# Attention and mixer on one core: channel weights with group scales, signs by GpSimd, norms by TensorE, and products of no use in the first batch

## The chip, the cores and the metric

The kernel runs on one core of a Trainium2 chip. The metric is device time in microseconds; each figure is a median of several runs. The core's engines are TensorE (PE in the views; PEld is its weight load), VectorE (DVE), ScalarE (ACT) and GpSimd (POOL); SyncE (SP) issues DMAs.

## What is computed

```python
def sm_attn(qq, kk, vv):                       # softmax attention, scale 1/8
    ...
q_d = q.reshape(B, H, S // 4, 4, D).mean(axis=3)      # the same for k, v
out_up = np.repeat(sm_attn(q_d, k_d, v_d), 4, axis=2)
scores = np.where(np.abs(pos[:, None] - pos[None, :]) < 4, q @ k.T / 8, -1e9)
out_local = softmax(scores) @ v
x = (out_up + out_local) as [B, S, H * D]
h = np.maximum(x^T @ w_tok1, 0) @ w_tok2
u = x + h^T
out = u + np.maximum(u @ w_ch1, 0) @ w_ch2
```

B, H, S, D are 8, 8, 576, 64, so x has 512 channels. `w_tok1` is 576x256, `w_tok2` 256x576, `w_ch1` 512x1536, `w_ch2` 1536x512. The weights are float64, all else is float32.

## The kernel before, in words

**Batches.** The eight batches run one after another. For each: queries and keys are pooled, four pairs of heads go through the pooled attention (`sd` scores, `pd`, `td` transposed, `ad` products, `od` output), five tiles of rows through the local one (`sc` scores, `P` exponentials, `mx` maxima, `r` sums, `pT` transposed, `av` products). `od` of all four pairs is written into the tile `vw` by DMAs on ACT's queue (L421), beside the windows of v, so that one `av` product adds both attentions; its result is `x`. The token mixer splits `x` into two parts (`xh`), forms `t` with W1 (five groups of six products, L105), `hid`, `t` again with W2 (L105, L545), `u`, and the maximum of `u` over all partitions (`um`: a reduction, a transpose on TensorE, a reduction, a product with ones). `u` is scaled by a power of two and split into two fp16 parts, `uh` (L567, L569). The channel mixer forms `c` from `uh` and C1, three products for the two parts each (`mm3`, L105), takes them up as `h` (relu, two fp16 parts, L644 and L646), and forms `c` from `h` and C2, which goes out as `u` (L672).

**Channel weights.** C1 and C2 have twelve tiles of 128x512 each. The chip reads float64 as pairs of 32-bit words. ACT scales the high word (L175), GpSimd rounds the low one (L178), DVE shifts the high word into it (L180) and, in `signed` (L184), ORs the sign bit in, into a tile of CW. TensorE multiplies the upper halves of the words by a matrix of ones, so that DVE (L283) finds the largest sum over a column. When all twelve tiles are there, one power of two for the whole matrix follows (`pow2`, L109 to L111), and each tile is split into a first part on ACT (L268) and a second on DVE (L270). W1 (five pieces) and W2 (four) go the same way but for the scale, and are split by L213 and L215.

**Buffers.** Raw pieces of W1, W2 and C1 share the five buffers `h`, with two loads in flight in each of the three streams; C2's raw tiles come in pairs in the two buffers `vw`, after batch 0's last `av`.

**Order.** Instructions run on each engine in the order in which the program issues them. For batch 0 and the start of batch 1, `drive` sets it: a list of streams (generators), whose steps name an engine, an estimated time and what they need. It keeps a clock for each engine and takes the earliest step that is ready, or one earlier in the list if it starts within PATIENCE of that one. From batch 1 on, the channel products are issued in fixed order, and attention and mixer of the next batch (`side`) are dealt out beside them (`tick`).

Of the kernel before, what the change touches and what calls it, by code (L numbers as in the profile page):

```python
# [10 lines left out]
U32 = mybir.dt.uint32  # L11
U8 = mybir.dt.uint8
# [4 lines left out]
NEG = -1.0e30  # L17
# [15 lines left out]
def tile_ups_attention_mixer(ctx, tc, qk, vw, vr, w1, w2, c1, c2, out):  # L33
# [14 lines left out]
    BUFS = dict(h=5, w=4, xh=3, x=5, u0=4, u1=8, uh0=4, uh1=4, qk=4, qd=1, vw=2, vd=1, pt=2, od=1, sm=10, sc=24)  # L48
# [19 lines left out]
    onesb = sb.tile([128, 128], BF16, name="onesb")  # L68
    nc.vector.memset(onesb, 1.0)
# [6 lines left out]
    masks = []  # L76
    for kind in range(3):
        m = sb.tile([128, WB], F32, name=f"mask{kind}")
        nc.gpsimd.memset(m, 0.0)
        for j in range(4):  # L80
            a = m[QB * j:QB * j + QB]
            select(a, 0, -1, 1, WB, NEG)
            select(a, 6, 1, -1, WB, NEG)
            if kind == 0 and j == 0:
                select(a, -3, 0, 1, WB, NEG)
            if kind == 2 and j == 1:
                select(a, QB + 2, 0, -1, WB, NEG)
        masks.append(m)
# [3 lines left out]
    nc.gpsimd.memset(rep, 1.0)  # L92
    for j in range(4):
        a = rep[QB * j:QB * j + QB]
        select(a, 0, 1, -4, QB // 4, 0.0)
        select(a, 3, -1, 4, QB // 4, 0.0)
# [21 lines left out]
    clock = dict.fromkeys("AGVPSD", 0.0)  # L118
# [13 lines left out]
    def fetched(nbytes):  # L132
        clock["D"] = max(clock["D"], now[0]) + nbytes / 230e3
        return clock["D"] + 2.0

    def drive(streams, until):

        items = [[g, next(g, None), 0.0] for g in streams]
        while until not in made:
# [14 lines left out]
            if e == "P" and ("uh", 0, 0) not in made:  # L154
                us *= 1.8
# [13 lines left out]
    def to_f32(raw, at):  # L169
# [6 lines left out]
        yield step("G", 0.1 + n * 0.0016)  # L176

        nc.gpsimd.tensor_scalar(lo, lo, 2.0 ** -29, -0.501, ALU.mult, ALU.add)  # L178
        yield step("V", 0.08 + n * 0.0012)
        nc.vector.scalar_tensor_tensor(lo, hi, 3, lo, ALU.logical_shift_left, ALU.bitwise_or)  # L180

    def signed(y, raw):
        words = raw.rearrange("p (n two) -> p n two", two=2)
        nc.vector.scalar_tensor_tensor(y, words[:, :, 1], 0x80000000, words[:, :, 0],  # L184
                                       ALU.bitwise_and, ALU.bitwise_or)

    def load_raw(src, n, name):
        raw = T([src.shape[0], 2 * n], U32, "h", f"{name}_raw")
        nc.sync.dma_start(raw, src)
        return raw, fetched(src.shape[0] * n * 8)  # L190

    def load_raws(srcs, name):

        t = T([128, len(srcs), 1024], U32, "vw", f"{name}_raws")
        for i, s in enumerate(srcs):
            nc.sync.dma_start(t[:, i], s)
        return [(t[:, i], fetched(2 ** 19)) for i in range(len(srcs))]

    def token_weight(pieces, fin, name):
        raws = {}  # L200
        yield step("S", 0.1)
        for i in range(min(2, len(pieces))):
            raws[i] = load_raw(*pieces[i], f"{name}{i}")
        for i, (src, n) in enumerate(pieces):
            raw, at = raws.pop(i)
            yield from to_f32(raw, at)
            yield step("V", 0.08 + n * 0.0012)
            m = raw.rearrange("p (n two) -> p n two", two=2)[:, :, 0]
            signed(m, raw)
# [6 lines left out]
            make((name, i), e)
            if i + 2 < len(pieces):
                raws[i + 2] = load_raw(*pieces[i + 2], f"{name}{i + 2}")
# [4 lines left out]
    CW = [sb.tile([128, 512], F32, name=f"CW{i}") for i in range(2 * NF + 1)]  # L223

    class Channel:


        def __init__(self, name, src, at, k, sums, pairs):
            self.name, self.src, self.at, self.k, self.sums, self.pairs = name, src, at, k, sums, pairs
            self.fin = []  # L230

        def bank_of(self, i):
            return "m" if i % (NF if self.pairs else 4) == 0 else ""

        def stage(self, *start):
            name = self.name
            yield step("S", 0.1, *start)
            if self.pairs:
                raws = load_raws(self.src[0:2], f"{name}0") + load_raws(self.src[2:4], f"{name}2")
            else:  # L240
                raws = [load_raw(self.src[i], 512, f"{name}{i}") for i in range(2)]
            self.mx = sb.tile([128, 4], F32, name=f"{name}_mx")
            for i in range(NF):
                raw, at = raws[i]
                yield from to_f32(raw, at)
                yield step("V", 0.68)
# [12 lines left out]
            self.inv = sb.tile([128, 1], F32, name=f"{name}_inv")
            self.s = sb.tile([128, 1], F32, name=f"{name}_s")  # L260
            yield step("V", 0.6, *([("C1", NF - 1)] if self.at else []))
            nc.vector.tensor_reduce(big, self.mx[:, :self.n], axis=AX.X, op=ALU.max)
            pow2(big, 2.0 ** -self.k, self.inv, self.s)
            for i in range(NF):
                y = CW[self.at + i + 1]
                f = CW[self.at + i].bitcast(F16).rearrange("p (a n) -> p a n", a=2)
                yield step("A", 0.72)
                nc.scalar.activation(f[:, 0], y, AF.Copy, scale=self.s)  # L268
                t = yield step("V", 0.75)
                nc.vector.scalar_tensor_tensor(f[:, 1], y, self.s, f[:, 0], ALU.mult, ALU.subtract)  # L270
                self.fin.append(f)
                make((name, i), t)

    def sums_c1(w, i, ab):

        if i % 4 == 0:
            w.bank = PM(f"C1_sum{i}")
        for d in range(4):
            nc.tensor.matmul(w.bank[:, 128 * (i % 4):128 * (i % 4) + 128], onesb, ab[:, 128 * d:128 * d + 128],
                             start=d == 0, stop=d == 3)  # L280
        if i % 4 == 3:
            w.n = i // 4 + 1
            return lambda: nc.vector.tensor_reduce(w.mx[:, w.n - 1:w.n], w.bank, axis=AX.X, op=ALU.max)  # L283
# [16 lines left out]
    ic = sb.tile([128, 1], F32, name="ic")  # L300
# [199 lines left out]
    def mix(st):  # L500

        b = st.b
        NT = len(TILES)

        def xf(t):
            return st.x[t].rearrange("p hp two d -> p (hp two d)")

        def split(t):
            n = TILES[t][1]
            xh = st.xh[t] = T([n, 2, 512], F32R, "xh", f"xh{b}_{t}")  # L510
            yield step("A", 0.62, ("x", b, t), *([("over", 0, 0)] if b == 1 else []))
            nc.scalar.copy(xh[:, 0], xf(t))  # L512
            yield step("V", 0.69)
# [5 lines left out]
        for t in range(NT):  # L519
# [3 lines left out]
            if t + 2 < NT:  # L523
                yield from split(t + 2)
# [302 lines left out]
```

## Time and profile before

| | before |
|---|---|
| median of 3 runs | 974.76 us (973.32 to 977.28) |
| the profiled execution's own time | 977.24 us |
| its span | 975.5 us |
| granted TensorE clock, mean of the span | 0.975 |
| PE busy | 907.9 us, 93% |
| DVE busy | 506.0 us, 52% |
| ACT busy | 301.1 us, 31% |
| POOL busy | 112.4 us, 12% |
| moved by DMA | 68.28 MB |

The shares are means over a span that has two kinds of stretch: the first batch, in which weights are prepared, and seven batches of the same work. The rows below name a time, a duration, an engine, a line, an operation, and output<-input with their shapes; in groups stand the count, the busy sum, the mean of one in ns, and the idle time of the engine ahead of them with what ended most of it.

### The profile page before, as it was taken

What the parts mean: (1) busy time and instruction counts of PE and PEld (TensorE: products, weight loads), DVE (VectorE), ACT (ScalarE), POOL (GpSimd) and SP (SyncE); (2) the same over time, 40 slices, a digit from 0 to 9 for tenths busy, and PEclk for the clock granted to TensorE, in tenths of its full rate; (3) what the DMA queues carried; (4) which work ended last, traced back from release to release, by engine and by line L of the source; (5) the groups of instructions that cost most, each with busy time, mean ns of one, the idle gap of its engine ahead of it and who ended that gap; (6) DMA issues with size and microseconds to landing.
All of it is one profiled execution on the core that took longest, in us unless ns stands there. A gap on an engine that the chain in (4) does not pass through costs nothing. (4 is left out here: it accounts for less than half of the span.)

```text
span 975.5 us, 25542 instructions
## 1 busy us (share of the span) xinstructions
PE 907.9 (93%) x11292; PEld 712.2 (73%) x11292; DVE 506.0 (52%) x1187; ACT 301.1 (31%) x627; POOL 112.4 (12%) x213
## 2 busy tenths in 40 slices
PE   5747789999999999999999999999999999999998
PEld 4634467778867778677877778777876778777876
DVE  7879899244645354724555354724645345533221
ACT  1544456212323232422333232422432222322110
POOL 7143500030030003000120003000120000000000
PEclk9976799999999999999999999999999999999999
DMA  8266610530025002500133002600034000000000
GB/s 225 96 234 239 217 31 2 159 90 21 26 61 158 22 8 76 168 7 21 38 107 100 15 14 72 171 1 28 20 84 140 15 15 20 18 2 21 18 12 28
DMA packets 28221, 68.28 MB, mean 70 GB/s; under 512 B 3504, under 2 KB 14000, under 8 KB 26864
## 3 DMA queue, kind: packets, MB, share of 16 engines
q1 hardware_dynamic: 25552, 64.30, 21.9%
q10 hardware_dynamic: 2560, 2.36, 0.9%
q8 instruction: 88, 1.44, 0.6%
q14 instruction: 21, 0.17, 0.1%
HBM read 54.85 MB, written 9.44 MB: 66 GB/s over the span
## 5 line engine op out<-in xcount | busy, mean ns | idle before, releaser
L105 PEld LDWEIGHTS <-CW 128*128 128x128 f16 x4608 | 435.7, 98 | 136.5 <-issue 15.3
L105 PE MATMUL c<-uh,CW 128*128 128x256 f16 (+1 forms) x2304 | 310.7, 288 | 7.0 <-DVE CW L270 4.4
L105 PE MATMUL c<-h,CW 128*128 128x256 f16 (+1 forms) x2304 | 304.5, 287 | 0.8 <-issue 0.7
L646 DVE SCALAR_TENSOR_TENSOR h<-c,h 128x256 f16<-128x256 f32 (+1 forms) x192 | 87.3, 455 | 133.0 <-ACT h L644 131.9
L644 ACT ACTIVATE h<-c 128x256 f16<-128x256 f32 (+1 forms) x192 | 78.4, 408 | 211.2 <-PE c L105 211.0
L344 POOL TENSOR_TENSOR vr<-vr 72x256 f32<-72x256 f32 x64 | 49.0, 765 | 489.4 <-DMA vr<-in_vr_dram 298.1
L672 DVE SCALAR_TENSOR_TENSOR u<-c,io,u 128x256 f32<-128x256 f32 (+1 forms) x64 | 33.0, 516 | 109.7 <-PE c L105 109.7
L554 DVE TENSOR_REDUCE umx<-t 128x1 f32<-128x256 f32 (+1 forms) x64 | 29.2, 457 | 84.5 <-ACT u L552 84.4
L105 PE MATMUL t<-W,hid 128*128 128x256 f32 (+1 forms) x384 | 71.6, 323 | 0.0
L105 PE MATMUL t<-xh,W 128*128 128x512 f32 (+1 forms) x240 | 68.2, 419 | 1.1 <-ACT x L480 0.8
L552 ACT COPY u<-t 128x256 f32<-128x256 f32 (+1 forms) x64 | 25.5, 398 | 119.9 <-PE t L105 119.6
L105 PEld LDWEIGHTS t<-W,hid 128*128 128x128 f32 x384 | 56.7, 200 | 2.6 <-DVE hid L531 0.3
L105 PEld LDWEIGHTS t<-xh,W 128*128 128x128 f32 (+1 forms) x240 | 43.6, 192 | 12.5 <-issue 2.5
L475 PE MATMUL av<-vw,pt 47*32 47x64 f32 x2304 | 37.1, 233 | 14.6 <-ACT pt L466 4.4
L480 ACT COPY x<-av 128x512 f32<-128x512 f32 (+1 forms) x40 | 23.3, 582 | 88.4 <-PE av L475 80.9
L475 PEld LDWEIGHTS av<-vw,pt 47*32 47x32 f32 x2304 | 28.9, 110 | 25.2 <-issue 11.4
L567 ACT ACTIVATE uh<-u,us 128x256 f16<-128x256 f32 (+1 forms) x64 | 29.6, 524 | 49.0 <-DVE us L111 45.0
L407 PE MATMUL ad<-vd,ptd 72*72 72x65 f32 x512 | 42.5, 240 | 0.1
L407 PEld LDWEIGHTS ad<-vd,ptd 72*72 72x72 f32 x512 | 40.5, 157 | 1.3 <-ACT ptd L401 0.4
L545 PEld LDWEIGHTS t<-ident,x 128*128 128x128 f32 (+1 forms) x160 | 22.4, 146 | 18.4 <-issue 9.1
L545 PE MATMUL t<-ident,x 128*128 128x128 f32 (+1 forms) x160 | 33.0, 287 | 2.3 <-DVE umx L554 2.3
L569 DVE SCALAR_TENSOR_TENSOR uh<-u,us,uh 128x256 f16<-128x256 f32 (+1 forms) x64 | 31.1, 537 | 7.6 <-ACT uh L567 7.6
(84 smaller groups left out, 802.6 us busy)
## 6 DMA issues: line engine op xcount, KB each, us to landing
qk<-in_qk_dram SPq DMA_DIRECT2D x32, 579.0 KB
vw<-in_vw_dram SPq DMA_DIRECT2D x32, 351.0 KB
vr<-in_vr_dram SPq DMA_DIRECT2D x64, 144.0 KB
C_raw<-in_c_dram SPq DMA_DIRECT2D x12, 512.0 KB
C_raws<-in_c_dram SPq DMA_DIRECT2D x12, 512.0 KB
out_dram<-u SPq DMA_DIRECT2D x32, 160.0 KB
out_dram<-u SPq DMA_DIRECT2D x32, 128.0 KB
vw<-od ACTq DMA_DIRECT2D x32, 72.0 KB
```

Of the source, the lines that this page charges most:

```text
L105: nc.tensor.matmul(ps, lhs(a), rhs(c), start=first and i == 0, stop=last and i == 2, **kw)
L344: nc.gpsimd.tensor_add(t[:, 0:2], t[:, 0:2], t[:, 2:4])
L407: nc.tensor.matmul(ps[:, g, par], pt[:, par, kg, G * g:G * g + G], st.vd[:, kg, 2 * pr + par], start=kg == 0, stop=kg == 1)
L475: nc.tensor.matmul(ps[QB * j:QB * j + QB, par, D * hp:D * hp + D], pt[p, hp, QB * j:QB * j + QB], st.vw[h][p, g, D * hp:D * hp + D], start ...
L545: nc.tensor.matmul(ps[:, o:o + n], xf(t)[:, 128 * c:128 * c + 128], ident[:n, :n], start=i == 0, stop=False, is_transpose=True, skip_group ...
L552: nc.scalar.copy(u, ps)
L554: nc.vector.tensor_reduce(umx[:, c:c + 1], ps, axis=AX.X, op=ALU.max, apply_absolute_value=True)
L567: nc.scalar.activation(t[:, 0], us[c], AF.Copy, scale=s)
L569: nc.vector.scalar_tensor_tensor(t[:, 1], us[c], s, t[:, 0], ALU.mult, ALU.subtract)
L644: nc.scalar.activation(ht[:, 0], ps, AF.Relu)
L646: nc.vector.scalar_tensor_tensor(ht[:, 1], ps, 0.0, ht[:, 0], ALU.max, ALU.subtract)
L672: nc.vector.scalar_tensor_tensor(us[c], banks[c], io, us[c], ALU.mult, ALU.add)
```

## The change

**Signs.** `signed` and its DVE pass are gone. In `to_f32` GpSimd makes a second pass, which turns the high word into the sign and writes it into the upper 16 bits of the low word, ahead of DVE's shift and OR; that operation now writes a channel tile straight to its place.

```diff
+        top = raw.bitcast(BF16).rearrange("p (n four) -> p n four", four=4)[:, :, 1]
...
         nc.gpsimd.tensor_scalar(lo, lo, 2.0 ** -29, -0.501, ALU.mult, ALU.add)
-        yield step("V", 0.08 + n * 0.0012)
-        nc.vector.scalar_tensor_tensor(lo, hi, 3, lo, ALU.logical_shift_left, ALU.bitwise_or)
-    def signed(y, raw):
...
+        nc.gpsimd.tensor_scalar(top, hi.bitcast(F32), 2.0 ** -126, 2.0 ** -126, ALU.mult, ALU.mult)
+        e = yield step("V", 0.08 + n * 0.0012, *needs)
+        nc.vector.scalar_tensor_tensor(lo if y is None else y(), hi, 3, lo, ALU.logical_shift_left, ALU.bitwise_or)
```

**Norms and scales.** TensorE multiplies each 128x128 block of a tile by itself, four products a tile in C1 and in C2, so that the sums are of squares and not of magnitudes. Each group of four C1 tiles gets its own power of two: a maximum over the group's sums, the chain `everywhere` to one number on all partitions (m, t, m1, b), and `root`. C2 has one chain, for which the three group maxima are scaled by the groups' C1 factors; its scale is then multiplied by each group's factor.

```diff
+                a = ab[:, 128 * d:128 * d + 128]
+                nc.tensor.matmul(self.banks[i // 4][:, 128 * (i % 4):128 * (i % 4) + 128], a, a, start=d == 0, stop=d == 3)
...
+            for q in range(NQ):
+                yield from self.norms(q)
+                big = yield from everywhere(f"C1_n{q}", self.mx[:, q:q + 1])
...
+                for i in range(4 * q, 4 * q + 4):
+                    yield from self.parts(i)
```

**Products of no use.** `keep_busy` multiplies a tile of ones and nothing reads the result: 14 products at the start, and up to eight where the planner sees TensorE wait before the second half of batch 0's `uh`, 80 in all. 22 of them stand ahead of the first `sd`. The planner no longer counts TensorE's early steps as 1.8 times as long.

```diff
+    def keep_busy(n):
+        if n:
+            ps = P1("busy")
+            for _ in range(n):
+                nc.tensor.matmul(ps, junk[:, :128], junk, start=True, stop=True)
...
-            if e == "P" and ("uh", 0, 0) not in made:
-                us *= 1.8
+            if e == "P" and ("uh", 0, 1) not in made and free["g"]:
+                keep_busy(min(8, int((t - clock["P"]) * 0.6 / 0.22)))
```

**Loads and order.** C1's raw tiles have six buffers of their own (`cw`), which later hold C2's tiles (CX, with CY for the last). The nine token pieces are loaded over the five `h` buffers as these come free; C2's first four raw tiles lie in the `qk` buffers, the others in `vw`. `mix` is four streams (splits, products, takes, scaled) where it was one, and `drive`'s list has another order. The masks are made once and copied, and `rep`, a constant, is a reduction of the identity on DVE. In the added code, L182 and L183 are GpSimd's two passes, L185 DVE's OR, L257 and L259 the split into parts, L614 is the second part of `uh`, L444 `od`, L485 to L487 `r` and `P`.

On DVE, where the second half of a C1 tile is first written (before: L270; names are output<-inputs, C_s is the scale). Before:

```order
L569 SCALAR_TENSOR_TENSOR uh_1_1_1274<-u_1_1_1196,us_1_1258,uh_1_1_1274 128x320
L184 SCALAR_TENSOR_TENSOR CW_198<-C_raws 128x512
L569 SCALAR_TENSOR_TENSOR uh_1_2_1281<-u_1_2_1213,us_1_1258,uh_1_2_1281 128x320
L270 SCALAR_TENSOR_TENSOR CW_176<-CW_177,C_s,CW_176 128x512
L569 SCALAR_TENSOR_TENSOR uh_1_3_1286<-u_1_3_1235,us_1_1258,uh_1_3_1286 128x320
L180 SCALAR_TENSOR_TENSOR C_raws<-C_raws 128x512
L270 SCALAR_TENSOR_TENSOR CW_177<-CW_178,C_s,CW_177 128x512
```

The same place of the changed kernel:

```order
L523 TENSOR_REDUCE C_n_m_1188<-C_n_t 1x1
L614 SCALAR_TENSOR_TENSOR uh_0_1_1200<-u_0_1_1078,us_0_1177,uh_0_1_1200 128x256
L248 TENSOR_SCALAR C_inv_121<-C_n_b 128x1
L250 TENSOR_SCALAR C_inv_121<-C_inv_121 128x1
L251 RECIPROCAL C_s_124<-C_inv_121 128x1
L614 SCALAR_TENSOR_TENSOR uh_0_2_1211<-u_0_2_1093,us_0_1177,uh_0_2_1211 128x256
L259 SCALAR_TENSOR_TENSOR CW_134<-CW_135,C_s_124,CW_134 128x512
L614 SCALAR_TENSOR_TENSOR uh_0_3_1217<-u_0_3_1107,us_0_1177,uh_0_3_1217 128x256
```

The first part stood beside `uh` of batch 0's second half, row 181 of DVE's program, and stands now beside the first half's, row 123. Ahead of it were 44 passes of L180 and L184 over channel tiles; now nine of L185.

On DVE, around `od` of batch 1's fourth pair. Before:

```order
L270 SCALAR_TENSOR_TENSOR CW_199<-CW_200,C_s,CW_199 128x512
L446 TENSOR_TENSOR P_164<-sc_4_1978,mask_125 64x2x4x38
L450 TENSOR_REDUCE mx_4_2099<-P_164 64x8
L451 TENSOR_TENSOR P_164<-P_164,mx_4_2099 64x8x38
L646 SCALAR_TENSOR_TENSOR h_1_9_2051<-c_0_1_10_2070,h_1_9_2051 128x320
L413 TENSOR_SCALAR rd_3_2096<-ad_3_2087 72x4
L414 RECIPROCAL rd_3_2096<-rd_3_2096 72x4
L415 TENSOR_TENSOR od_1627<-ad_3_2087,rd_3_2096 72x4x64
L456 TENSOR_REDUCE r_4_2120<-P_164 64x8
```

Of the changed kernel:

```order
L259 SCALAR_TENSOR_TENSOR CX_1392<-CX_1393,C_s_133,CX_1392 128x512
L442 TENSOR_SCALAR rd_3_2233<-ad_3_2224 72x4
L443 RECIPROCAL rd_3_2233<-rd_3_2233 72x4
L444 TENSOR_TENSOR od_1872<-ad_3_2224,rd_3_2233 72x4x64
L259 SCALAR_TENSOR_TENSOR CX_1393<-CX_1393,C_s_133 128x512
L485 TENSOR_REDUCE r_3_2267<-P_110 128x8
L486 RECIPROCAL r_3_2267<-r_3_2267 128x8
L487 TENSOR_TENSOR P_110<-P_110,r_3_2267 128x8x38
L259 SCALAR_TENSOR_TENSOR CX_1393<-CY_1394,C_s_133,CX_1393 128x512
```

C2's last two parts and the `r` rows of tiles 3 and 4 stood ahead of `od` and stand now behind it.

On GpSimd, at C2's and C1's last tiles (C_raw without a number is a buffer of `cw`). Before:

```order
L178 TENSOR_SCALAR C_raw<-C_raw 128x512 x2
L178 TENSOR_SCALAR C_raws<-C_raws 128x512 x2
L178 TENSOR_SCALAR C_raw<-C_raw 128x512 x2
L178 TENSOR_SCALAR C_raws<-C_raws 128x512 x3
L322 MEMSET vd_1472 72x16
```

Of the changed kernel:

```order
L182 TENSOR_SCALAR C_raws_937<-C_raws_937 128x512
L183 TENSOR_SCALAR C_raws_937<-C_raws_937 128x512
L182 TENSOR_SCALAR C_raws_937<-C_raws_937 128x512
L183 TENSOR_SCALAR C_raws_937<-C_raws_937 128x512
L182 TENSOR_SCALAR C_raw<-C_raw 128x512
L183 TENSOR_SCALAR C_raw<-C_raw 128x512
```

C1's last tiles alternated with C2's in twos, one pass each; now eight tiles of C2 (the last of them shown), each with two passes, stand ahead of C1's last three.

More of the change, by code (lines that the diff above doesn't have):

```diff
@@ L73, in select @@
                                 fill=fill, base=base, channel_multiplier=cm)
[L76 to L88, printed above, removed]
-    rep = sb.tile([128, QB // 4], F32, name="rep")
[L92 to L96, printed above, removed]
+    masks = [sb.tile([128, WB], F32, name=f"mask{kind}") for kind in range(3)]
+    m = masks[1]
+    nc.gpsimd.memset(m, 0.0)
+    for j in range(4):
+        a = m[QB * j:QB * j + QB]
+        select(a, 0, -1, 1, WB, NEG)
+        select(a, 6, 1, -1, WB, NEG)
+    for kind, j, base, step_ in ((0, 0, -3, 1), (2, 1, QB + 2, -1)):
+        nc.gpsimd.tensor_copy(masks[kind], m)
+        select(masks[kind][QB * j:QB * j + QB], base, 0, step_, WB, NEG)
+    rep = sb.tile([128, QB // 4], F32, name="rep")
+    nc.vector.tensor_reduce(rep, ident.rearrange("p (j m f) -> p m j f", j=4, f=4), axis=AX.XY, op=ALU.add)
     PT = [sb.tile([128, H, 64], F32, name=f"P{i}") for i in range(3)]
@@ L182, in signed @@
-    def signed(y, raw):
[L183 to L197, printed above, removed]
@@ L216, in token_weight @@
[L216 to L218 removed]
+            yield step("S", 0.1, *([(name, "read", i - BUFS[tag])] if i >= BUFS[tag] else []))
+            raws[i] = T([src.shape[0], 2 * n], U32, tag, f"{name}{i}_raw")
+            nc.sync.dma_start(raws[i], src)
+            made[name, "raw", i] = fetched(src.shape[0] * n * 8)
+            made[name, "raw"] = raws
+    def token_weight(i, n, f):
+        yield step("A", 0.0, ("W", "raw", i))
+        raw = made["W", "raw"][i]
+        yield from to_f32(raw, made["W", "raw", i])
+        y = raw.rearrange("p (n two) -> p n two", two=2)[:, :, 0].bitcast(F32)
+        yield step("A", 0.1 + n * 0.0011)
+        nc.scalar.copy(f[:, 0], y)
+        e = yield step("V", 0.08 + n * 0.0012)
+        nc.vector.tensor_tensor(f[:, 1], y, f[:, 0].bitcast(F32), ALU.subtract)
+        make(("W", "y", i), e)
+        make(("W", "read", i), e)
@@ new lines, in splits @@
+        def splits():
+            for t in range(NT):
+                n = TILES[t][1]
+                yield step("A", 0.62, ("x", b, t), *([("over", 0, 0)] if b == 1 else []),
+                           *([("t1", b, t - 3)] if t > 2 else []))
+                xh = st.xh[t] = T([n, 2, 512], F32R, "xh", f"xh{b}_{t}")
+                nc.scalar.copy(xh[:, 0], xf(t))
+                e = yield step("V", 0.69)
+                nc.vector.tensor_tensor(xh[:, 1], xf(t), xh[:, 0].bitcast(F32), ALU.subtract)
+                make(("xh", b, t), e)
@@ L574, in together @@
+        return [splits(), products(), takes(), scaled()]
     def together(todo, most):
@@ L600, in ahead @@
     def ahead(b):
-        yield step("S", 0.1, *([("mixed", 0)] if b == 1 else []))
+        yield step("S", 0.1, *([("C2", "read", i) for i in range(4)] if b == 1 else []))
         st = load(b)
@@ L608, in ahead @@
         if b == 1:
-            yield step("S", 0.1, ("C2", "rough"))
+            yield step("S", 0.1, *(("C2", "read", i) for i in range(4, NF)))
             load_w(st)
@@ L618, in side @@
             if b + 1 < B:
-                yield from together([m, ahead(b + 1)], 2)
-            else:
-                yield from m
+                m.append(ahead(b + 1))
+            yield from together(m, len(m))
     def first(st, ch, places):
@@ L700, in attend, with mix_of @@
                 + [lazily(lambda t=t: local(ready[b], t), ok) for t in range(len(TILES))])
+    mixes = {}
+    def mix_of(b):
+        if b not in mixes:
+            mixes[b] = mix(ready[b])
+        return mixes[b]
     def windows(st):
```

344 lines of the change are left out of this document (184 added, 160 removed).

## The prediction

> **What bounds the kernel now.** I read the page's slices first, then a table of windows, the timeline of the turning point, the waits, and the groups of instructions.
>
> ```profile
> PE   5747789999999999999999999999999999999998
> PEclk9976799999999999999999999999999999999999
> ```
>
> Each digit is one fortieth of the span (24.4 us). TensorE is full from the seventh slice on; what is lost lies in the first seven, where its clock is lower too. The chain of work that ended last is printed only back to 809 us, so it says nothing of this stretch; the windows do:
>
> ```profile
> 0.00:50.00 50.00, 31.87 (x702) 26.62 (x702) 37.12 (x93) 17.19 (x33) 19.61 (x66) 1.00 0.60 162
> 50.00:110.20 60.20, 37.13 (x185) 25.31 (x185) 51.27 (x93) 26.32 (x54) 21.91 (x30) 0.70 0.69 256
> 110.20:171.30 61.10, 54.62 (x717) 40.76 (x718) 58.04 (x123) 34.82 (x66) 13.73 (x17) 0.93 0.15 33
> 171.30:225.00 53.70, 52.15 (x642) 41.21 (x640) 17.00 (x37) 10.42 (x20) 9.62 (x16) 0.97 0.41 119
> 225.00:850.00 625.00, 610.16 (x8125) 484.06 (x8123) 309.37 (x767) 189.66 (x404) 47.57 (x85) 1.00 0.19 55
> 850.00:975.50 125.50, 121.97 (x930) 94.25 (x927) 33.19 (x77) 22.73 (x53) 0.00 (x0) 1.00 0.05 16
> ```
>
> The columns are the window, its length, then busy time of PE, PEld, DVE, ACT and POOL, the granted clock, DMA share and GB/s. From 171 us TensorE is 97 to 98% busy. Before that DVE is the fuller engine: 51.3 of 60.2 us, then 58.0 of 61.1. Its busy time up to 171.3 is 146.4, its idle time 24.9, of which 12.9 fall in the first 50 us.
>
> Why 171.3:
>
> ```profile
> 170.92 0.42 DVE L415 TENSOR_TENSOR od<-ad,rd 72x256 f32<-72x256 f32 x1
> 171.26 0.46 DVE L456 TENSOR_REDUCE r<-P 64x8 f32<-64x312 f32 x1
> 171.37 3.19 ACTq L421 DMA_DIRECT2D vw<-od  x4
> 171.75 0.20 DVE L457 RECIPROCAL r<-r 64x8 f32<-64x8 f32 x1
> 171.99 0.47 DVE L458 TENSOR_TENSOR P<-P,r 64x304 f32<-64x304 f32 x1
> 172.38 0.48 DVE L646 SCALAR_TENSOR_TENSOR h<-c,h 128x320 f16<-128x320 f32 x1
> 174.86 0.27 PE L475 MATMUL av<-vw,pt 47*32 47x64 f32 x2 [1.04 <-DMA vw<-od]
> ```
>
> DVE writes batch 1's last pooled output (`od`), a DMA puts it into `vw`, and TensorE waits for that DMA before batch 1's first `av`. Behind it the order of TensorE is nearly the same in both kernels, and TensorE is full. So I price the change by how much earlier DVE ends this **mark**, the `od` row of pair 3 of batch 1; the rest moves along with it.
>
> **The change, part by part.** First what DVE has to do ahead of the mark.
>
> ```profile
> L184 DVE SCALAR_TENSOR_TENSOR CW<-C_raw 128x512 uint32<-128x512 uint32 x12 | 9.4, 781 | 0.2
> L184 DVE SCALAR_TENSOR_TENSOR CW<-C_raws 128x512 uint32<-128x512 uint32 x12 | 9.2, 767 | 0.2
> L184 DVE SCALAR_TENSOR_TENSOR W_raw<-W_raw 128x256 uint32<-128x256 uint32 x4 | 2.0, 508 | 0.1
> L184 DVE SCALAR_TENSOR_TENSOR W_raw<-W_raw 128x288 uint32<-128x288 uint32 x4 | 1.8, 454 | 0.1
> L283 DVE TENSOR_REDUCE C_mx<-C_sum 128x1 f32<-128x512 f32 x3 | 2.0, 682 | 0.0
> L494 DVE TENSOR_REDUCE um_m<-um_t 1x1 f32<-1x128 f32 x2 | 0.5, 270 | 0.0
> L488 DVE TENSOR_REDUCE um_m<-umx 128x1 f32<-128x4 f32 x2 | 0.3, 158 | 0.1
> L111 DVE RECIPROCAL C_s<-C_inv 128x1 f32<-128x1 f32 x2 | 0.3, 164 | 0.1
> ```
>
> Gone: the pass that puts the sign in, 9.4 + 9.2 + 2.0 + 1.8 = **22.4 us** (the ninth token piece, smaller, is left out).
>
> Added: six maxima over the product sums for four, 2 x 0.68 = 1.4. Four chains to one number for all partitions (m 0.16, m1 0.27, three scalars of some 0.16, 0.9 together), 3.6, for two short ones of 0.6, so +2.4. Six small scalings of some 0.16, 0.9. `rep` by DVE, a reduction over 128 elements, which the trace does not have: between 0.16 (L488, 4 elements) and 0.46 (L456, 312), 0.3 taken. Together **+5.0**.
>
> Moved behind the mark: the last two parts of C2 (0.83 each by the L270 row below), the three `r` rows of tile 3 (1.1, as above) and three of tile 4 (some 0.46 each, 1.4), while one `h` row (0.48) comes ahead: **-3.5**, counting a part as 0.74. They are covered by the DMA of 3.2 us and the two `av` products; without that cover 3.5 us return.
>
> Then what GpSimd takes over. A second operation per piece, 33 in all, whose form (float32 in, 16-bit words out) the trace lacks.
>
> ```profile
> L178 POOL TENSOR_SCALAR C_raws<-C_raws 128x512 uint32<-128x512 uint32 x12 | 9.9, 827 | 16.9 <-DMA C_raws<-in_c_dram 11.8 <-ACT u L552 4.5
> L178 POOL TENSOR_SCALAR C_raw<-C_raw 128x512 uint32<-128x512 uint32 x12 | 9.4, 787 | 15.2 <-DMA C_raw<-in_c_dram 14.9
> L178 POOL TENSOR_SCALAR W_raw<-W_raw 128x288 uint32<-128x288 uint32 x4 | 2.6, 642 | 1.0 <-DMA W_raw<-in_w_dram 0.7
> L178 POOL TENSOR_SCALAR W_raw<-W_raw 128x256 uint32<-128x256 uint32 x4 | 1.8, 443 | 25.6 <-DMA W_raw<-in_w_dram 25.6
> L270 DVE SCALAR_TENSOR_TENSOR CW<-CW,C_s,CW 128x512 f16<-128x512 f32 x24 | 19.9, 830 | 0.1
> ```
>
> ```profile
> 111.30 0.95 DVE L270 SCALAR_TENSOR_TENSOR CW<-CW,C_s,CW 128x512 f16<-128x512 f32 x1
> 113.45 1.16 POOL L344 TENSOR_TENSOR vr<-vr 72x256 f32<-72x256 f32 x1
> 113.96 1.21 DVE L270 SCALAR_TENSOR_TENSOR CW<-CW,C_s,CW 128x512 f16<-128x512 f32 x1
> 117.52 0.73 POOL L344 TENSOR_TENSOR vr<-vr 72x256 f32<-72x256 f32 x1
> 128.40 0.74 DVE L270 SCALAR_TENSOR_TENSOR CW<-CW,C_s,CW 128x512 f16<-128x512 f32 x1
> ```
>
> Its price lies between L178 (0.80 for 512 elements, one input) and twice L344 alone (0.73 for 256 elements of two inputs, so 1.46); I take L178's, the same shape and kind, so 9.9 + 9.4 + 2.6 + 1.8 = 23.7 us more of GpSimd. GpSimd was busy 21.9 and 13.7 us of the 121 between 50 and 171, so it has room. What counts is what it takes from DVE: L270 lasts 0.74 beside an idle GpSimd and 1.21 beside the addition that itself grew from 0.73 to 1.16. Lower bound: if L270's mean of 0.83 against 0.74 is all that GpSimd costs now, 24 x 0.09 = 2.2 us are lost over its 35.6 us, 0.06 us per us, so 1.5. Upper: every microsecond costs what that pair does, 0.47 / 1.16 = 0.40, so 9.5. Neither row is nearer, since every second DVE operation there is of L270's kind; I take **+6**, near the middle of 5.5. [...]
>
> Then waiting.
>
> ```profile
> 105.51 0.16 DVE L488 TENSOR_REDUCE um_m<-umx 128x1 f32<-128x4 f32 x1
> 107.34 0.16 DVE L111 RECIPROCAL us<-ui 128x1 f32<-128x1 f32 x1
> ```
>
> ```profile
> DVE W_raw L180 <- POOL W_raw L178: 4.1, 3, 3.0
> PE sd L380 <- DVE qd L368: 7.1, 3, 6.2
> ```
>
> DVE loses the 4.1 us in which it stood for token pieces that were loaded late (all five `h` buffers are now filled at once, and C1 has six of its own). It gains four chains that take 2.0 us each from m to reciprocal, 0.9 of it work, so up to 1.1 of waiting each, 4.4 where nothing else stands between; the order puts conversions between most, so 3. Net **-1**, with bounds of -8 (the 8.9 us of DVE idle in the second window nearly gone) and +8 (as much again, since the token pieces no longer fill the pauses of attention).
>
> Costed at nothing: the products for the norms (as many columns as before, and TensorE has 23 us idle in the second window); the fewer mask steps; the steady batches, where the four streams of the mixer are dealt out in another order: 14.8 us of TensorE's 625 are idle there, so it can win some 4 and lose as much. The 80 products of no use: the nearest rows are six products of 512 columns,
>
> ```profile
> 53.13 2.93 PE L105 MATMUL t<-xh,W 128*128 128x512 f32 x6
> 206.31 1.68 PE L105 MATMUL t<-xh,W 128*128 128x512 f32 x6
> ```
>
> 0.49 each in a slow stretch and 0.28 in a fast one, so 22 to 39 us beside 18.1 and 23.1 us of idle. 22 of them stand before the first score, where TensorE waits 6.2 us for DVE in any case: 22 x 0.28 = 6.2 fits, 22 x 0.49 = 10.8 makes attention up to 4.6 late. What they win is the slow clock, half the price of the token products; it shortens DVE's waits, within the -8 above.
>
> **Sum**: -22.4 + 5.0 - 3.5 + 6 - 1 = **-16 us**. Against the profiled execution's 977.24 us (span 975.5 and 1.7 around) this gives 961; that execution is 2.5 above the median of 974.76, so I forecast **959**. Its own range: contention 1.5 to 9.5, and half of the idle bounds either way, 951 to 967.
>
> **The rivals.**
>
> *More than that* (0.16): the waits fall by the 8 and contention stays at 1.5: -22.4 + 5.0 - 3.5 + 1.5 - 8 = -27, 947 by the median. For it: the slow clock makes DVE wait in 50 to 110 us. Against: attention has less beside it.
>
> *GpSimd locks DVE out for its whole length* (0.13): the term is 23.7, the sum +1.7, 976, no change. [...]
>
> *The useless products do not keep the clock* (0.08): the token products stay at 0.49. The five groups of six of the first mixer stand on the way to the first channel product: (2.93 - 1.68) x 5 = 6, and the second ones as much, so 12 of waiting: 971.
>
> *Slower* (0.08): GpSimd becomes the bound. It works in order, and the last C1 tile stands behind nine token pieces and 19 tiles, eight of them C2's.
>
> ```profile
> 27.24 0.42 POOL L178 TENSOR_SCALAR W_raw<-W_raw 128x256 uint32<-128x256 uint32 x1 [6.98 <-DMA W_raw<-in_w_dram]
> ```
>
> From 27.2 us the old operations take 9 x 0.55 + 20 x 0.80 = 21, and the new ones, p for a tile and 0.6 p for a piece, 25.4 p: the last C1 tile is ready at 48 + 25.4 p. DVE wants it some 12 us of rows after the first part (L270), which was at 111.3 and comes 31 us earlier (35 fewer conversions of 0.77 and nine of 0.45 ahead of it): at 92. At p = 0.80 there are 23 us to spare; from 1.7 DVE waits, from 2.4 the 16 us are gone, and at 2.6 the time is 981. Against: p lies beyond both bounds.
>
> **Numbers.** 0.55 for the forecast. 0.5% (4.9 us) is about what a measurement here can tell from no change. Faster: the forecast, more than that, and a third of the slow-clock rival, 0.74; within 0.5%: the lock and the rest of that, 0.18; slower 0.08. The range of 945 to 975 leaves out the slower rival and little of the others.
>
> **What would show it.** Right: no DVE sign pass and some 24 us more of GpSimd; L259 (once L270) below 0.9 on the mean; the mark at 155 us; the first channel product near 80; clock 0.9 or more in 50 to 110; TensorE idle as before after the mark. Wrong: the new GpSimd operation above 1.5 us; L259 near 1.2; DVE idle above 30 us ahead of the mark; or a mark that is early with an end that isn't, which would put the loss into the later batches.

## The result, and the profile after

The changed kernel takes 990.54 us (median of four runs) against 975.88. One of the four took 1512.81 us at a clock of 0.55 and is left out of the ratio; the other three took 987.09 to 992.10. The ratio is 1.0128, interval 1.0093 to 1.0163, so some 12.5 us slower (0.0128 x 976). The profiled execution took 988.98 us, 11.7 more than the one profiled before, with a span of 987.0. The forecast was 959, with 945 to 975 as its range.

The page of the changed kernel, three rows of its slices (24.7 us each):

```profile
PE   6766897799999999999999999999999999999998
POOL 5359434021020003000020003000030000000000
PEclk9778998699999999999999999999999999999999
```

TensorE is full from the ninth slice on, where it was from the seventh; GpSimd is now busy through the third to fifth. The windows of the changed kernel, cut at its mark (`od` of pair 3 of batch 1), with the columns as before (window, length, busy time of PE, PEld, DVE, ACT, POOL, clock, DMA share, GB/s):

```profile
0.00:50.00 50.00, 34.57 (x602) 21.30 (x603) 34.64 (x88) 14.94 (x29) 24.15 (x52) 0.88 0.74 207
50.00:110.00 60.00, 42.63 (x369) 29.80 (x369) 32.39 (x62) 30.11 (x61) 44.18 (x41) 0.82 0.36 132
110.00:179.20 69.20, 60.70 (x781) 47.94 (x780) 62.35 (x140) 32.34 (x60) 21.97 (x29) 0.90 0.35 104
225.00:850.00 625.00, 609.46 (x8042) 484.74 (x8041) 306.66 (x760) 186.83 (x397) 48.09 (x87) 1.00 0.20 55
```

DVE did lose work: up to the mark it is busy 34.6 + 32.4 + 62.4 = 129.4 us, 17.0 less than before. But it now stands idle for 179.2 - 129.4 = 49.8 us, 24.9 more, most of that in 50 to 110 us, where it is busy half of the time. GpSimd is busy 44.2 of those 60 us. The steady stretch is as it was, 15.5 us of TensorE idle for 14.8.

The timeline of the changed kernel at the mark (start, duration, engine, line, operation; in brackets the idle time ahead and what ended it):

```profile
178.84 0.42 DVE L444 TENSOR_TENSOR od<-ad,rd 72x256 f32<-72x256 f32 x1
179.34 2.94 ACTq L450 DMA_DIRECT2D vw<-od  x4
182.82 0.39 PE L504 MATMUL av<-vw,pt 47*32 47x64 f32 x2 [4.15 <-DMA vw<-od]
```

The mark came at 179.26 and not at 155: 7.9 us later than before. TensorE then stands 4.15 us for the DMA, where it stood 1.04: it had no channel products left to do meanwhile. So the mark explains 7.9 of the 11.7 us, and this wait 3.1 more.

What the operations cost, from the groups of the changed kernel:

```profile
L183 POOL TENSOR_SCALAR C_raw<-C_raw 128x512 bf16<-128x512 f32 x16 | 23.8, 1486 | 21.3 <-ACT C_raw L179 20.3
L183 POOL TENSOR_SCALAR C_raws<-C_raws 128x512 bf16<-128x512 f32 x8 | 11.9, 1486 | 8.1 <-ACT C_raws L179 7.7
L182 POOL TENSOR_SCALAR C_raw<-C_raw 128x512 uint32<-128x512 uint32 x16 | 13.6, 850 | 1.3
L259 DVE SCALAR_TENSOR_TENSOR CW<-CW,C_s,CW 128x512 f16<-128x512 f32 x12 | 10.9, 912 | 1.0 <-ACT CW L257 0.8
L259 DVE SCALAR_TENSOR_TENSOR CX<-CX,C_s 128x512 f16<-128x512 f32 x6 | 4.5, 744 | 0.4 <-ACT CX L257 0.3
L259 DVE SCALAR_TENSOR_TENSOR CX<-CX,C_s,CX 128x512 f16<-128x512 f32 x5 | 3.7, 746 | 0.1
```

The sign pass takes 1.49 us a tile, where I took 0.80. DVE's second parts (L259) are as long as before: with the twenty-fourth (0.75) 19.9 us for 24, a mean of 0.83.

Where DVE's idle time comes from, first by the timeline of DVE of the changed kernel:

```profile
78.67 0.69 DVE L185 SCALAR_TENSOR_TENSOR CW<-C_raw 128x512 uint32<-128x512 uint32 x1 [0.47 <-POOL C_raw L183]
79.28 0.42 DVE L595 TENSOR_REDUCE umx<-t 128x1 f32<-128x256 f32 x1
81.32 0.69 DVE L185 SCALAR_TENSOR_TENSOR CW<-C_raw 128x512 uint32<-128x512 uint32 x1 [1.63 <-POOL C_raw L183]
81.93 0.42 DVE L595 TENSOR_REDUCE umx<-t 128x1 f32<-128x256 f32 x1
83.97 0.69 DVE L185 SCALAR_TENSOR_TENSOR CW<-C_raw 128x512 uint32<-128x512 uint32 x1 [1.62 <-POOL C_raw L183]
```

The order puts one conversion of a C1 tile ahead of each maximum of `u` (L595). GpSimd delivers a tile every 2.65 us, so DVE does 1.1 us of work and waits 1.6, and batch 0's `u`, its scale and the first C1 part (99.60 us, forecast 80) come at GpSimd's pace. The planner had counted 1.69 us for the two passes; by the groups above they take 0.85 + 1.49. Part of the 2.65 is contention: GpSimd's first pass, which starts just behind DVE's L185 here, is longer than where no L185 runs beside it.

```profile
81.37 1.14 POOL L182 TENSOR_SCALAR C_raw<-C_raw 128x512 uint32<-128x512 uint32 x1
89.33 0.65 POOL L182 TENSOR_SCALAR C_raw<-C_raw 128x512 uint32<-128x512 uint32 x1
```

Second, TensorE's timeline in the same kernel, at three places:

```profile
19.14 0.28 PE L436 MATMUL ad<-vd,ptd 72*72 72x65 f32 x1
25.13 1.95 PE L436 MATMUL ad<-vd,ptd 72*72 72x65 f32 x15 [5.71 <-issue]
46.80 1.94 PE L504 MATMUL av<-vw,pt 47*32 47x64 f32 x119 [0.89 <-DMA vw<-od]
51.30 0.43 PE L504 MATMUL av<-vw,pt 47*32 47x64 f32 x7 [2.55 <-issue]
53.98 1.54 PE L504 MATMUL av<-vw,pt 47*32 47x64 f32 x109
59.98 0.64 PE L504 MATMUL av<-vw,pt 47*32 47x64 f32 x19 [4.45 <-issue]
```

Three times it stops inside a group of like products, waiting for nothing that the profile shows: 5.7, 2.6 and 4.5 us. The products up to these stops number 222, 602 and 730: the last two are 128 apart, the first two 380 (three times 128 less four missing records). 128 products are 256 instructions, weight loads included. Around each stop one packet of 16 KB passes in the DMA queue that the page lists as instruction (89 packets, 1.46 MB in the whole span). So I take these to be ends of code blocks of 256 instructions: my reading of the count and the packets, since no view shows what TensorE stands for there. The first stop shows on DVE as a wait of 5.1 us ahead of L442, for `ad`. In the last stop the others stand too:

```profile
55.50:60.00 4.50, 0.05 (x6) 0.02 (x4) 0.05 (x1) 0.21 (x1) 0.00 (x0) 0.79 1.01 387
```

The DMA engines are full (1.01), with C1's and C2's tiles; all five engines are nearly idle.

### The profile page after: what moved, and what is told of

Same layout as the page of the kernel before. It is cut to its first block, busy times and chain, and to the rows that moved or that the text cites. A ratio compares the mean times of both kernels' runs of the same rounds, so it can differ in the third digit from the quotient of the medians.

```text
span 987.0 us, 25805 instructions
## 1 busy us (share of the span) xinstructions
PE 920.5 (93%) x11420; PEld 718.0 (73%) x11420; DVE 492.4 (50%) x1174; ACT 302.1 (31%) x627; POOL 147.5 (15%) x221
## 3 DMA queue, kind: packets, MB, share of 16 engines
q8 instruction: 89, 1.46, 0.6%
## 5 line engine op out<-in xcount | busy, mean ns | idle before, releaser
L101 PE MATMUL c<-uh,CW 128*128 128x256 f16 (+1 forms) x2304 | 306.9, 286 | 2.6 <-DVE h L691 2.4
L101 PE MATMUL c<-h,CX 128*128 128x256 f16 (+1 forms) x2304 | 306.6, 288 | 1.9 <-issue 1.8
L101 PEld LDWEIGHTS <-CW 128*128 128x128 f16 x2304 | 217.5, 98 | 68.9 <-issue 15.2
L101 PEld LDWEIGHTS <-CX 128*128 128x128 f16 x2304 | 219.9, 99 | 61.9 <-issue 3.4
L689 ACT ACTIVATE h<-c 128x256 f16<-128x256 f32 (+1 forms) x192 | 78.5, 409 | 221.8 <-PE c L101 221.6
L101 PE MATMUL t<-W,hid 128*128 128x256 f32 (+1 forms) x384 | 68.8, 315 | 0.9 <-ACT hid L580 0.6
L595 DVE TENSOR_REDUCE umx<-t 128x1 f32<-128x256 f32 (+1 forms) x64 | 29.3, 457 | 72.7 <-ACT u L593 72.7
L101 PEld LDWEIGHTS t<-W,hid 128*128 128x128 f32 x384 | 54.3, 191 | 3.5 <-ACT hid L580 0.8
L101 PEld LDWEIGHTS t<-xh,W 128*128 128x128 f32 (+1 forms) x240 | 43.5, 191 | 12.3 <-issue 2.3
L546 DVE TENSOR_TENSOR xh<-x,xh 128x512 fp32r<-128x512 f32 (+1 forms) x40 | 27.9, 698 | 21.1 <-ACT xh L544 21.1
L614 DVE SCALAR_TENSOR_TENSOR uh<-u,us,uh 128x256 f16<-128x256 f32 (+1 forms) x64 | 31.8, 540 | 9.0 <-ACT uh L612 9.0
```

Of the source, the lines that this page charges most:

```text
L101: nc.tensor.matmul(ps, lhs(a), rhs(c), start=first and i == 0, stop=last and i == 2, **kw)
L546: nc.vector.tensor_tensor(xh[:, 1], xf(t), xh[:, 0].bitcast(F32), ALU.subtract)
L595: nc.vector.tensor_reduce(umx[ch][:, c:c + 1], ps, axis=AX.X, op=ALU.max, apply_absolute_value=True)
L614: nc.vector.scalar_tensor_tensor(t[:, 1], st.u[ch][c], s, t[:, 0], ALU.mult, ALU.subtract)
L689: nc.scalar.activation(ht[:, 0], ps, AF.Relu)
```

## The experiments

Three theories. **A**: GpSimd's second pass, at 1.49 us, sets the pace. **B**: the stops at code blocks delay batch 0's attention, because the products of no use shift the blocks' ends and the loads fill the DMA engines. **D**: the products of no use cost their own time. A refinement of A came with the runs: not GpSimd's work, but an order that is planned for less of it. The table has the ratio to the kernel before with its interval, the mark, and from the waits DVE's time ahead of `xh` (for ACT, which follows TensorE's `av`) and ahead of C1's L185 (for GpSimd). Mark and waits (up to 165 us) are those of one profiled execution each, the ratio is over all runs. The profiled executions of e3, e4, e6, e7, e10 and e11 were the fastest of their runs, those of e9 and e12 the second slowest, so a mark and a ratio in one line need not belong together. A run is named by the start of its label (e8) below.

| run | ratio | mark | `xh` | L185 |
|---|---|---|---|---|
| changed kernel | 1.0128 (1.0093 to 1.0163) | 179.3 | 11.7 | 6.6 |
| e1_no_sign | 1.0034 (1.0013 to 1.0056) | 168.6 | 13.6 | none |
| e2_few_loads | 1.0199 (1.0174 to 1.0223) | 193.7 | 7.3 | 5.8 |
| e3_no_junk | 1.0057 (1.0031 to 1.0083) | 167.3 | 3.7 | 6.1 |
| e4_sign_by_dve | 1.0123 (1.0097 to 1.0149) | 177.2 | 2.3 | none |
| e5_narrow_junk | 1.0105 (1.0057 to 1.0152) | 174.6 | 10.1 | 6.6 |
| e6_aligned_junk | 1.0135 (1.0107 to 1.0163) | 171.6 | 2.2 | 6.6 |
| e7_no_junk_sign_by_dve | 1.0106 (1.0077 to 1.0134) | 174.9 | 3.4 | none |
| e8_no_junk_true_cost | 0.9971 (0.9955 to 0.9986) | 163.3 | 3.9 | 1.2 |
| e9_true_cost_with_junk | 1.0007 (0.9984 to 1.0030) | 171.6 | 11.5 | 3.3 |
| e10_pass_32bit | 1.0087 (1.0054 to 1.0119) | 170.3 | 12.3 | 0.8 |
| e11_no_junk_sign_by_dve_planned | 1.0011 (0.9993 to 1.0030) | 168.4 | none | none |
| e12_qk_free | 1.0030 (1.0002 to 1.0058) | 168.8 | 3.7 | 1.2 |

**The sign pass left out.**

```diff
-        nc.gpsimd.tensor_scalar(top, hi.bitcast(F32), 2.0 ** -126, 2.0 ** -126, ALU.mult, ALU.mult)
```

> GpSimd's second pass (the sign) is left out, so the weights count without their sign; every other instruction and the order are those of the changed kernel. Theory A (pace): that pass takes 1.49 us a tile, 43 us in all, and makes GpSimd the engine that DVE waits for from 63 to 113 us. Then GpSimd falls from 147 to about 104 us busy, DVE's idle time ahead of od of pair 3 of batch 1 (the mark) falls from 50 us to about 30, the mark comes from 179 to 165 or earlier, and the time from 990 to 978 or less. Theory B (code): TensorE stands three times (5.7, 2.8 and 4.6 us) at the end of a block of 256 instructions while the DMA engines are full of C1's and C2's loads, and the others stand behind it. Then the three pauses stay, and the time stays within 5 us of 990.

The mark moved to 168.6, 10.6 us earlier, and the ratio fell by 0.94 points, 9.2 us: the way A has it, though short of its 978 (981.18) and its mark of 165. The stops stayed (4.8, 2.7 and 4.4 us, by TensorE's weight loads), and the time fell all the same, which B did not allow. But A's mechanism is only a part of it. The windows up to the mark, changed kernel and this run:

```profile
0.00:179.26 179.26, 137.90 (x1752) 99.04 (x1752) 129.44 (x288) 77.45 (x150) 90.30 (x120) 0.87 0.46 142
0.00:168.62 168.62, 135.74 (x1752) 98.09 (x1752) 122.22 (x288) 77.38 (x150) 46.79 (x87) 0.88 0.48 151
```

The same 288 operations of DVE take 7.2 us less: that is what GpSimd's pass cost DVE by contention. DVE's idle time falls only from 49.8 to 46.4, where A expected 30: the wait for GpSimd is gone, and that for `xh` is 1.9 longer.

**Fewer loads in flight.**

```diff
-            yield step("S", 0.1, *([(name, "read", i - BUFS[tag])] if i >= BUFS[tag] else []))
+            yield step("S", 0.1, *([(name, "read", i - 2)] if i >= 2 else []))
```

> Token pieces and C1 tiles are loaded two at a time, as before the change; the planner deals the work out anew around that. Theory B (code): with fewer loads in flight TensorE's pauses of 5.7, 2.8 and 4.6 us shrink to below 1.5 us each, and the time falls by 8 to 13 us, to 977 to 982. Theory A (pace): GpSimd's 43 us more stay, DVE waits for it in 63 to 113 us as now, and the time stays within 5 us of 990 whatever the pauses do.

Neither came. The planner dealt out another order, in which TensorE's weight loads once stand 13.6 us for W's split. The first stop was 6.4 us, and up to 75 us no other of more than 0.6 is left. As the order changed with the loads, the run decides nothing between A and B.

**No products of no use.**

```diff
-        if n:
+        if False:
             ps = P1("busy")
```

> The 80 products of no use are left out, the order of all else is that of the changed kernel. If they keep the clock as meant, the granted clock in 0 to 110 us falls from 0.85 to about 0.7 and the time rises by 5 us or more. If they only stand in the way (22 of them ahead of the first score), it falls by 3 to 6 us. Theories A and B both leave room for either; each expects less than 5 us either way, since TensorE is not what the mark waits for in 63 to 113 us.

0.71 points less, 6.9 us: more than either theory allowed. The clock in 50 to 110 us stayed (0.83 without them, 0.82 with), and in the first 50 us it was higher without them (1.00 for 0.88; 0.89 in e7, also without), so the granted clock shows no gain from them. TensorE's own rows do, at the start: the first eight `sd` products, behind 22 of them, took 0.71 us, and 1.24 behind 22 narrow ones (e5). The groups of the changed kernel give their own time as 25.6 us for the 80.

**The sign as a pass of DVE, same order.**

```diff
         nc.vector.scalar_tensor_tensor(lo, hi, 3, lo, ALU.logical_shift_left, ALU.bitwise_or)
+        nc.vector.scalar_tensor_tensor(lo if y is None else y(), hi, 0x80000000, lo, ALU.bitwise_and, ALU.bitwise_or)
```

with GpSimd's second pass gone.

> The sign goes back to DVE as a pass of its own behind its OR; GpSimd has one pass again; the order is otherwise that of the changed kernel. Theory A (pace): GpSimd falls to about 104 us busy, DVE gains 22 us of work, most of which fits into its 50 us of idle time ahead of the mark: the mark at 168 to 174, the time at 978 to 984. Theory B (code): the pauses stay and DVE has 22 us more to do: 990 to 1000.

The wait for GpSimd is gone, and DVE's 22 us fill the room: up to the mark DVE is busy for 146.6 us, 17 more than in the changed kernel, and idle for 30.6, 19 less. Nothing is gained that the intervals can tell; 988.26 lies above A's 978 to 984 and below B's 990 to 1000.

**Blocks or their own time: the products one column wide, then 48 more of these.** The first keeps the places of the blocks and drops the work, the second keeps the work and moves the blocks back.

```diff
-                nc.tensor.matmul(ps, junk[:, :128], junk, start=True, stop=True)
+                nc.tensor.matmul(ps[:, :1], junk[:, :128], junk[:, :1], start=True, stop=True)
```

> The 80 products of no use keep their places and their number of instructions, but have 1 column in place of 512, so they take next to no time and cannot keep the clock. Theory B (code): what they cost is that they shift the ends of the code blocks (after 222, 602 and 730 products) onto work beside full DMA engines: the pauses of 5.7, 2.8 and 4.6 us stay within 1.5 us of these and the time stays near the changed kernel's, 986 to 992. Theory D (their own time): they hold attention up: the time falls to that without them, 980 to 984, whatever the pauses do.

```diff
         keep_busy(14)
+        ps = P1("busy")
+        for _ in range(48):
+            nc.tensor.matmul(ps[:, :1], junk[:, :128], junk[:, :1], start=True, stop=True)
```

> The 80 products stay as they are and 48 more with 1 column each are put behind the first 14, so that the products of use lie 128 products (one block of code) further than without any, at the same places within the blocks as in the kernel without products of no use. Theory B (code): the pauses go back to below 2 us each, as there (1.5, 1.1 and 1.3 us), and the time to 979 to 984. Theory D (their own time): the time stays at 988 to 992.

The stops followed the blocks. With narrow products the second and third stayed (2.5 and 3.6 us by TensorE's weight loads; the first fell below 1), with the blocks moved back all three are below 1.2. From the waits of DVE, narrow products first, then moved blocks:

```profile
DVE xh L546 <- ACT xh L544: 10.1, 3, 5.9
```

```profile
DVE xh L546 <- ACT xh L544: 2.2, 2, 1.9
```

So DVE's wait of some 10 us ahead of `xh` belongs to the stops, not to the products' own time. The times do not settle it. With narrow products 987.93 lies in B's 986 to 992; with the blocks moved back 989.96 lies in D's 988 to 992, where B expected 979 to 984. TensorE's timeline with the blocks moved back shows one reason, in the profiled execution:

```profile
148.15 0.74 PE L468 MATMUL sc<-qk 64*32 64x38 f32 x60 [0.94 <-ACT ptd L430]
152.56 0.34 PE L468 MATMUL sc<-qk 64*32 64x38 f32 x4 [3.67 <-issue]
```

Another stop of 3.7 us falls on batch 1's attention, ahead of the mark; loads run beside its start, but the DMA share is down to 18% from 150 to 151 us and 7% from 151 to 152, so full DMA engines do not explain its length. B is right that the stops follow the blocks; how the cost of the products divides between stops and their own time is not shown by these two runs.

**Neither products nor GpSimd's sign.** Both edits above, in the order of the changed kernel.

> No products of no use, and the sign as a pass of DVE, in the order of the changed kernel. If both costs are separate and add (8.0 and 2.3 us by the runs with one of them), 980. Theory A (pace): with the pauses of TensorE gone GpSimd's 43 us are the bound, so that taking them away is worth more than beside the pauses: 974 to 977. If DVE is the bound then, its 22 us more cost: 984 or more.

987.67: the last branch. Up to its mark DVE is busy 16.2 us more than in e3 and idle 8.6 less, and the mark comes 7.6 later (174.9 for 167.3).

**The planner told the true cost**, without the products and then with them:

```diff
-        yield step("G", 0.2 + n * 0.0029)
+        yield step("G", 0.2 + n * 0.0042)
```

> No products of no use, and the planner is told what the two passes of GpSimd take (2.35 us a tile of 512 where it had 1.69); GpSimd keeps the sign. If the loss is in the order (DVE and ACT stand in a row in which a conversion comes before GpSimd has done its part), the time falls from 982 to 976 to 979. If GpSimd's sheer work is the bound, it stays at 980 to 985.

> The changed kernel with its products of no use, but the planner is told what GpSimd's two passes take (2.35 us a tile of 512 in place of 1.69). If order and products of no use are two separate costs (7.6 us between the two runs without these products, 8.0 between the two orders' first and the changed kernel), the time is 982 to 984. If the order only matters where TensorE's early work is on time, it stays at 987 or more. If it repairs both, 975.

No other edit has so large an effect. GpSimd does nearly the same work, 146 to 149 us, yet the ratio falls by 0.86 points without the products (8.4 us) and by 1.21 with them (11.8). The waits of DVE in e3 and in e8:

```profile
DVE CW L185 <- POOL C_raw L183: 6.1, 5, 1.6
DVE xh L546 <- ACT xh L544: 3.7, 2, 3.1
```

```profile
DVE xh L546 <- ACT xh L544: 3.9, 2, 3.2
DVE CW L185 <- POOL C_raw L183: 1.2, 1, 1.2
```

Of these two waits only the one for GpSimd shrinks, by 4.9 us, and the mark comes 4.0 earlier. That these two executions lie 1.7 us apart (975.86 and 974.15), and the medians 7.6, leaves open where the rest went. The pair with the products is closer to its medians: up to the mark DVE is busy 129.9 us in e9 for 129.4, and idle 41.7 for 49.8. Of these 8.1 us less, 3.3 are the wait for GpSimd and 3.8 the wait for `ad` (1.3 for 5.1), since in the new order the first stop falls elsewhere. The first C1 part comes at 90.9 us in place of 99.6. So the true cost brings back 11.8 of the 12.5 us; that all of it is GpSimd's pace is not shown, as a new order also moves the ends of the blocks. e9 came out below its 982 to 984: the products cost 0.36 points beside this order and 0.71 beside the other, and the two costs do not simply add.

**What makes the pass dear.** In place of 16-bit words it writes 32-bit ones (the high word times 1; the sign is left out).

```diff
-        nc.gpsimd.tensor_scalar(top, hi.bitcast(F32), 2.0 ** -126, 2.0 ** -126, ALU.mult, ALU.mult)
+        nc.gpsimd.tensor_scalar(hi.bitcast(F32), hi.bitcast(F32), 1.0, 1.0, ALU.mult, ALU.mult)
```

> GpSimd's second pass writes 32-bit words in place (the high word times 1) instead of 16-bit words; the sign is left out with it, the order is that of the changed kernel. If its price lies in the 16-bit output, the pass takes 0.73 to 0.85 us a tile in place of 1.49, and the time comes near the one without the pass: 981 to 985. If it lies in the float32 input, the pass stays at 1.4 to 1.5 us and the time at 988 to 992.

```profile
L183 POOL TENSOR_SCALAR C_raw<-C_raw 128x512 f32<-128x512 f32 x16 | 13.4, 838 | 25.2 <-ACT C_raw L179 24.5
```

0.84 us for 1.49, with the same input, so the price does not lie in the float32 input. Both forms write every 8 bytes, 16-bit words there and 32-bit words here; the factors differ too (2^-126 twice there, 1 here), and the two were not told apart. The time is 987.91 (980 to 991), above the 981 to 985 expected, and its interval overlaps that of the changed kernel. The profiled execution, the fastest of eight, took 979.87, with the first C1 part at 91.7 us and a wait for GpSimd of 0.8, much as e1 (980.24) and e9 (981.41). Here GpSimd's two passes take 0.81 + 0.84, about the 1.69 that the planner had counted, and yet the median stays high: that plan and price agree was not enough, and what the slower executions lost is not shown.

**The sign by DVE, with the order planned for it.** As e7, with 0.1 + n x 0.0016 for GpSimd's step and 0.16 + n x 0.0026 for DVE's.

> No products of no use, the sign by DVE, and the planner is told so (GpSimd 0.92, DVE 1.49 us a tile). If the sign on GpSimd is worth its place once the order fits, this is slower than the run with the sign there and the true cost (974.9): 978 to 984. If the order is all, it is within 2 us of that: 973 to 977.

978.96 against 974.89: 0.40 points. With an order that fits, the sign is better on GpSimd; the order alone is worth 0.95 points here (e7 to e11).

**Batch 1's loads earlier**, on top of e8: C2's tiles all go into `vw`, and `ahead` waits for the first mixer only.

```diff
-                if i < 4:
...
+                if i % 2 == 0:
+                    yield step("S", 0.1, *(("av", 0, t) for t in range(len(TILES))), *([("C2", "read", i - 4), ("C2", "read", i - 3)] if i >= 4 else []))
+                    two = T([128, 2, 1024], U32, "vw", f"C2_raws{i}")
+                t = two[:, i % 2]
...
-        yield step("S", 0.1, *([("C2", "read", i) for i in range(4)] if b == 1 else []))
+        yield step("S", 0.1, *([("mixed", 0)] if b == 1 else []))
...
-            yield step("S", 0.1, *(("C2", "read", i) for i in range(4, NF)))
+            yield step("S", 0.1, *(("C2", "read", i) for i in range(NF)))
```

> No products of no use, true cost, and C2's first four raw tiles go into the vw buffers as before the change, so that batch 1's queries and keys need not wait in the qk buffers for DVE to have read them. If batch 1's late loads are what leaves TensorE short of work in 140 to 170 us (8 us idle, clock 0.50 to 0.67), the loads of qk come by 85 us in place of 105 to 112, od of pair 3 of batch 1 by 160, and the time falls from 974.9 to 968 to 972. If C2's parts are what it lacks there, they come later still, and the time rises to 977 or more.

The loads of qk came at 70 us in place of 104, and the mark later (168.8), the ratio 0.59 points higher. So earlier loads alone did not help. Nor did C2's parts come later, as the other branch has it: DVE wrote them from 140.7 to 168.9 us, in e8 from 146.3 to 170.7. In this order TensorE stops for 2.9 us at 143 and for 3.3 more at 179 and 187, waiting for nothing that the profile shows, where e8 has one such stop of 0.8 between 100 and 200; this may hide a gain.

## Why the prediction was wrong

- **DVE's work** was right: -22.4 + 5.0 - 3.5 + 6 = -14.9 forecast, -17.0 measured. Within it the contention came near: the 6 taken stand against 7.2 by e1. That is luck in part, since 0.25 us was taken for each of 23.7 us of GpSimd, and 7.2 us for 43 us is 0.17. L259's mean does not show it: over all 24 parts it stayed at 0.83, but it is 0.91 for C1's twelve and 0.75 for C2's, which came after GpSimd's passes. Single pairs slow each other: L259 took 1.46 and 1.48 us beside GpSimd's passes (L183, 1.38 and 1.45 us there and 1.33 at the least), and 0.74 at 105.73 us, though a pass ran there too, to 106.07. Only three of the first twelve parts lie above 1. No run shows the term of 23.7, with which one rival has DVE locked out for all of GpSimd's added time: e1 shows 7.2 us for 43.
- **The step that failed is the waiting**, "Net -1, with bounds of -8 and +8": it was +24.9. The trace names 11.7 of `xh`, 6.6 of L185 and 5.1 of `ad`, where before there was 4.1 for token pieces, 1.2 for `ad` and none for `xh`. The 6.6 are GpSimd's pace; the 11.7 and the 5.1 go with TensorE's stops (2.2 of `xh` in e6, 1.4 of `ad` in e3). I counted waits by what stood where in the old trace, and did not ask which row of the new order would wait for GpSimd.
- **GpSimd's price** was mis-sized: 0.80 taken, bounds to 1.46, 1.49 measured, so 43 us of GpSimd in place of 23.7. Of the rows at hand the dearer was nearer.
- **The rival that GpSimd becomes the bound** had the right engine and the wrong point. It priced only the last C1 tile, at 48 + 25.4 p = 86 us for p = 1.49, and let GpSimd run without waiting. That tile was ready at 114, since GpSimd itself stood for ACT: ACT's L179 for that tile began at 111.83 us, behind an L689 that had waited 2.07 us for TensorE. The waits of GpSimd, changed kernel:

```profile
POOL C_raw L183 <- ACT C_raw L179: 20.3, 4, 9.9
POOL W_raw L183 <- ACT W_raw L179: 9.6, 3, 7.5
```

  And DVE waited for the middle tiles, at 78 to 87 us, because each conversion stands ahead of a row of batch 0's `u`. So "from 1.7 DVE waits" was wrong: it waited at 1.49.
- **The products of no use** were costed at nothing. They cost 6.9 us in the changed kernel and 3.5 with the better order. I looked for their cost ahead of the first score; much of DVE's wait came at what I take for ends of code blocks, of which the prediction said nothing.
- **The mark** as what sets the end held in part: 7.9 of 11.7 us. Behind it TensorE had run dry and stood for the DMA, "covered by the DMA of 3.2 us" with nothing to do under it. Nor does the rest move along with the mark: from it to the end of the span the profiled executions take 800 (e2) to 814 us (e12), 804.2 before the change.
- **The clock** rose from 0.70 to 0.82 in 50 to 110 us and not to 0.9, and just as far without the products. In the first 50 us it fell from 1.00 to 0.88, so that over 0 to 110 us it is 0.84 in both kernels.

What stays open: e8, the fastest version here (0.9971, 974.89 us), has its mark 8.0 us ahead of the kernel before, and gains 2.8 us. From the mark to the end of the span it takes 972.3 - 163.3 = 809.0 us, the kernel before 975.5 - 171.3 = 804.2. Its windows show where:

```profile
140.00:170.00 30.00, 23.27 (x351) 17.69 (x350) 23.75 (x56) 13.56 (x23) 4.03 (x8) 0.61 0.22 55
```

TensorE is short of work for 6.7 us there, at a clock of 0.61, while C2's parts are being made. The kernel before has TensorE busy for 29.98 us of the same stretch. That C2 coming late is the reason was not tried.

## What to carry to other kernels

When work moves to an engine that has room, ask not only whether it fits by its sum but which row of each engine's order will stand behind it, and give the planner the measured price: the same kernel was 8 to 12 us faster when one number in it was right. Ask too what the pass takes from the engine beside it: 7 us of DVE here. Price an operation whose form the trace lacks by the dearer bound until it has been measured. Instructions that do nothing can still change where TensorE stops: 48 narrow products more took stops of 5.7, 2.6 and 4.5 us to below 1.2 here, and one of 3.7 us came elsewhere.

## What the runs showed of the hardware

- A GpSimd operation of 128x512 took 1.49 us on the mean (1.33 at the least) with 16-bit output every 8 bytes, and 0.84 with 32-bit output every 8 bytes, from the same float32 input; the factors differed as well.
- GpSimd's 43 us of that pass lengthened the same 288 operations of DVE by 7.2 us together (129.4 and 122.2), and a GpSimd pass of 0.65 us took 1.14 just behind an operation of DVE.
- TensorE stopped after 222, 602 and 730 products, whole numbers of 128 products (256 instructions) apart but for four missing records: for 5.7, 2.6 and 4.5 us in the changed kernel beside C1's and C2's loads (DMA share 1.06, 0.73 and 1.01), and for 1.2 and 1.4 us after 222 and 730 products in e8, which has no products of no use, though the DMA engines were full around the second there as well (0.99 from 51.3 to 55.5 us). Between 222 and 602 products no such stop of more than 0.7 us inside a group shows. What sets the length was not found.
